# A gated MLP computed in rows instead of columns, and the last rows of its output weight loaded over another weight, beside a decode attention

## The chip, the cores and the metric

One core of a Trainium2 chip. The time is device microseconds of one execution, the median of three runs. The profile is one execution of its own, taken by the hardware profiler. TensorE (PE) multiplies matrices, VectorE (DVE) and ScalarE (ACT) work on lanes, GpSimd (POOL) fills constants, and SyncE (SP) issues nearly all transfers (DMA) in one order.

## The reference, cut to what matters

For four batch rows of 640 values, the output is the input plus an attention over cached keys and values plus a gated MLP, both of the normalised input.

```python
x = A_x                                  # (4, 1, 640)
xn = _layernorm(x)
# attention: 32 heads of 128, 4096 cached positions
q = xn @ wq                              # wq (640, 4096)
p = softmax(q . k_cache * 128 ** -0.5)   # k_cache (4, 32, 4096, 128)
a = (p @ v_cache) @ wo
# gated MLP: F = 1728, Fh = 864
z = _gelu(xn @ w_in)                     # w_in (640, 1728)
z1, z2 = z[..., :Fh], _layernorm(z[..., Fh:])
g = w_sp * z2 + b_sp                     # S = 1: one number each
return x + a + (z1 * g) @ w_out          # w_out (864, 640)
```

The caches are 134 MB each and bfloat16. All weights together are about 14 MB.

## The kernel before, in words

**Units.** The attention is cut into `NU` = 16 units, one batch row and eight heads each. A unit's keys and its values are 8.39 MB each. Keys come in four quarters (`NK`) of 64 KB by 128 lanes in total, into `ring` (shown as k_ring), seven places of a quarter each. Values go to `v_all`, which holds one unit.

**One quarter of keys** (`product`, `fold_half`, `sums`, called by the loop at the end with a running number n): DVE multiplies the quarter by the broadcast query (L537), adds its halves (L543), and PE sums the rest by eight products with the identity (L555). After the sums the ring place is free. `row_sums`, `head_max`, `exps` and `by_head` make the weights of a unit; `weighted` (L631) multiplies them with the values.

**Order of the transfers.** `loads` is a list written out by hand. `pump` goes along it and issues on SP until an entry needs a place that is still in use. The first call of `pump` comes right after the list, before the normalisation and the query products are written down. It issues: unit 0's first and second key quarters, `load_w` (w_in and w_out's large parts), unit 0's other two quarters, `load_w_few` (w_out's 12-lane part). Unit 1's keys need the ring place that unit 0's first quarter holds, so they wait for the `sums` of that quarter. Unit 0's values need `v_all`, marked V, which is freed after the MLP's last step. The tile framework keeps the order in which reads and writes of one place are written down: a later access waits for an earlier one. It also lets transfers take turns on eight completion counters, and a transfer waits for the one eight before it on its counter.

**Places at the start.** `v_all` is first a store for weights: wq in columns 0 to 20,479, w_in in 20,480 to 29,119, then the five-row part of w_out. The other parts of w_out lie in `p_buf` (shown as p_m), which later holds the attention's weights.

**The start of the work.** x comes in by ACT's queue. DVE normalises it (L265 to L274), PE transposes it (L289), and 40 products with wq (L303) make the queries, copied out by L311. `stage_q` spreads a unit's query over the lanes (L519, L527), and the loop begins.

**The MLP** (`gmlp`) is a generator whose pieces the loop places between the first two quarters' steps: after n = 0 the products, after the fold of n = 1 the polynomial and the tanh and the gate with the lane sums, after the sums of n = 1 the statistics, the scale and the output products, and then `v_all` is freed. Before, the MLP has the features on lanes: 140 products (L404) with pieces of w_in as weights give 14 columns by 4 batch rows on up to 128 lanes for each half. The elementwise steps work on 112 values a lane (L414 to L432). The statistics of the normalisation come from a product with ones, a reduction on one lane (L435 to L473), and a product that sends them back to all lanes (L482). L503 multiplies the result with w_out's 14 parts, in two halves of 320 columns each.

Of the kernel before, what the change touches and what calls it, by code (L numbers as in the profile page):

```python
# [9 lines left out]
FP32 = mybir.dt.float32  # L10
BF16 = mybir.dt.bfloat16
# [6 lines left out]
def kernel(  # L18
# [40 lines left out]
    RW = 8  # L59
    QW = HC * Dh  # L60
    RING = 2 * NK - 1
    W_OUT = ((P, 5, 1), (P, 1, 1), (12, 8, 4))
    assert sum(n * r for n, r, _ in W_OUT) == Fh
    NFC = sum(r for _, r, _ in W_OUT)

    def up(n):
        return -(-n // 256) * 256

    PW = sum(up(r * D) for _, r, _ in W_OUT[1:])
    NOH = D // 2  # L70
    CB = 4
    NG = NR // CB
# [26 lines left out]
    ring = places.tile([P, RING, QW], BF16, name="k_ring")  # L99
    x_bf = ring[0:Bsz, 1, 0:D]  # L100
    nc.scalar.dma_start(out=x_bf, in_=A_x.flatten_outer_dims())
    v_all = places.tile([P, NK * QW], BF16, name="v_all")

    wq_sb = v_all[:, 0 : DC * HD].rearrange("p (c n) -> p c n", c=DC)
# [1 line left out]


    at_v = up(DC * (HD + F))
    w_parts, f0, at_p = [], 0, 0
    for n, r, t in W_OUT:  # L110
        if f0 == 0:
            room = v_all[0:n, at_v : at_v + r * D]
        else:
            room = p_buf[0:n, at_p : at_p + r * D]
            at_p += up(r * D)
        w_parts.append((room.rearrange("p (k n) -> p k n", k=r), f0, n, r, t))
        f0 += n * r
    nc.sync.dma_start(out=wq_sb, in_=A_wq.rearrange("(p c) n -> p c n", c=DC))

    def load_part(part):  # L120
        w, f0, n, r, t = part
        rows = B_w_out[f0 : f0 + n * r].rearrange("(p k) n -> p k n", k=r)
        for l in range(t):
            nc.sync.dma_start(out=w[l:n:t], in_=rows[l:n:t])

    def load_w():
        nc.sync.dma_start(out=w_in_sb, in_=B_w_in.rearrange("(p c) n -> p c n", c=DC))
        for part in w_parts:
            if part[4] == 1:
                load_part(part)  # L130

    def load_w_few():
        for part in w_parts:
            if part[4] > 1:
                load_part(part)

    w_rows = [
        (w[:, i], f0 + i, n, r) for w, f0, n, r, _ in w_parts for i in range(r)
    ]

    def run_of(cache, u):
        hg, b = divmod(u, Bsz)
# [137 lines left out]
        op1=ALU.mult,  # L280
    )

    wsp_bf = const.tile([1, 1], BF16)
    bsp_bf = const.tile([1, 1], BF16)

    xn_v = xn_bf.rearrange("b (p c) -> b c p", c=DC)
    xnT_ps = ps_m.tile([P, DC, Bsz], BF16, tag="m")
# [90 lines left out]
            stop=False,  # L378
        )

    gm = {}
    for name in ("zz", "gw", "gt"):
        gm[name] = work.tile([P, 2, NFC, Bsz], FP32, name=name)
    gm["gz"] = work.tile([P, 3, NFC, Bsz], FP32, name="gz")
    nc.gpsimd.memset(gm["zz"][:], 0.0)
    gm["st"] = work.tile([1, 5 * Bsz], FP32, name="st")
    gm["ac"] = work.tile([1, 2 * Bsz], FP32, name="ac")
    gm["yT"] = work.tile([P, NFC, Bsz], BF16, name="yT")

    by_lanes = []  # L390
    for n, r, _ in W_OUT:
        if by_lanes and by_lanes[-1][0] == n:
            by_lanes[-1] = (n, by_lanes[-1][1] + r)
        else:
            by_lanes.append((n, r))

    def gmlp():
        zz, gw, gt, gz = (gm[n] for n in ("zz", "gw", "gt", "gz"))
        zT = ps_pv.tile([P, 2, NFC, Bsz], FP32, tag="pv", name="zT")
        for t in range(2):  # L400
            w_t = w_in_sb[:, :, t * Fh : (t + 1) * Fh]
            for k, (_, f, n, r) in enumerate(w_rows):
                for c in range(DC):
                    nc.tensor.matmul(  # L404
                        out=zT[0:n, t, k, :],
                        lhsT=w_t[:, c, f : f + (n - 1) * r + 1 : r],
                        rhs=xnT[:, c, 0:Bsz],
                        start=(c == 0),
                        stop=(c == DC - 1),
                    )  # L410
        yield
        k0 = 0
        for n, ks in by_lanes:
            nc.vector.tensor_copy(  # L414
                out=zz[0:n, :, k0 : k0 + ks, :], in_=zT[0:n, :, k0 : k0 + ks, :]
            )
            k0 += ks
        nc.vector.tensor_tensor(out=gw[:], in0=zz[:], in1=zz[:], op=ALU.mult)
        nc.vector.tensor_scalar(
            out=gw[:], in0=gw[:], scalar1=0.044715, scalar2=1.0, op0=ALU.mult, op1=ALU.add  # L420
        )
        nc.vector.tensor_tensor(out=gw[:], in0=gw[:], in1=zz[:], op=ALU.mult)
        nc.scalar.activation(
            out=gt[:], in_=gw[:], func=ACT.Tanh, scale=math.sqrt(2.0 / math.pi)
        )
        yield
        nc.vector.tensor_scalar(
            out=gt[:], in0=gt[:], scalar1=1.0, scalar2=0.5, op0=ALU.add, op1=ALU.mult
        )
        nc.vector.tensor_tensor(out=gz[:, 0:2], in0=zz[:], in1=gt[:], op=ALU.mult)  # L430
        sq = gz[:, 2, :, :]
        nc.vector.tensor_tensor(out=sq, in0=gz[:, 1, :, :], in1=gz[:, 1, :, :], op=ALU.mult)  # L432

        s_ps = ps_m.tile([1, 2, NFC, Bsz], FP32, tag="m", name="ln_ps")
        nc.tensor.matmul(  # L435
            out=s_ps[:], lhsT=ones_sq[:, 0:1], rhs=gz[:, 1:3], start=True, stop=True
        )
        yield
        st, ac = gm["st"], gm["ac"]
        mean_t = st[:, 0:Bsz]  # L440
        ex2_t = st[:, Bsz : 2 * Bsz]
        var_t = st[:, 2 * Bsz : 3 * Bsz]
        rst_t = st[:, 3 * Bsz : 4 * Bsz]
        tmp_t = st[:, 4 * Bsz : 5 * Bsz]
        nc.vector.tensor_reduce(
            out=st[:, 0 : 2 * Bsz].rearrange("o (s b) -> o s b", s=2),
            in_=s_ps[:].rearrange("o s k b -> o s b k"),
            axis=AX.X,
            op=ALU.add,
        )  # L450
        nc.vector.tensor_scalar(
            out=st[:, 0 : 2 * Bsz],
            in0=st[:, 0 : 2 * Bsz],
            scalar1=1.0 / float(Fh),
            scalar2=None,
            op0=ALU.mult,
        )
        nc.vector.tensor_tensor(out=tmp_t, in0=mean_t, in1=mean_t, op=ALU.mult)
        nc.vector.tensor_tensor(out=var_t, in0=ex2_t, in1=tmp_t, op=ALU.subtract)
        nc.scalar.activation(  # L460
            out=rst_t, in_=var_t, func=ACT.Sqrt, bias=eps_tile[:1], scale=1.0
        )
        wsp_t = work.tile([1, 1], FP32, name="wsp_t")
        nc.gpsimd.tensor_copy(out=wsp_t[:], in_=wsp_bf[:])
        bsp_t = work.tile([1, 1], FP32, name="bsp_t")
        nc.gpsimd.tensor_copy(out=bsp_t[:], in_=bsp_bf[:])
        yield
        nc.vector.reciprocal(out=rst_t, in_=rst_t)
        nc.vector.tensor_scalar(
            out=ac[:, 0:Bsz], in0=rst_t, scalar1=wsp_t[:, 0:1], scalar2=None, op0=ALU.mult  # L470
        )
        nc.vector.tensor_tensor(out=tmp_t, in0=ac[:, 0:Bsz], in1=mean_t, op=ALU.mult)
        nc.vector.tensor_scalar(  # L473
            out=ac[:, Bsz : 2 * Bsz],
            in0=tmp_t,
            scalar1=-1.0,
            scalar2=bsp_t[:, 0:1],
            op0=ALU.mult,
            op1=ALU.add,
        )  # L480
        ac_ps = ps_m.tile([P, 2 * Bsz], FP32, tag="m", name="ac_ps")
        nc.tensor.matmul(  # L482
            out=ac_ps[:], lhsT=ones_sq[0:1, :], rhs=ac[:], start=True, stop=True
        )
        ac_sb = work.tile([P, 2 * Bsz], FP32, name="ac_sb")
        nc.scalar.copy(out=ac_sb[:], in_=ac_ps[:])
        yield
        nc.vector.tensor_tensor(
            out=sq,
            in0=gz[:, 1, :, :],  # L490
            in1=ac_sb[:, None, 0:Bsz].to_broadcast([P, NFC, Bsz]),
            op=ALU.mult,
        )
        nc.vector.tensor_tensor(
            out=sq,
            in0=sq,
            in1=ac_sb[:, None, Bsz : 2 * Bsz].to_broadcast([P, NFC, Bsz]),
            op=ALU.add,
        )
        nc.vector.tensor_tensor(out=gm["yT"][:], in0=gz[:, 0, :, :], in1=sq, op=ALU.mult)  # L500
        for k, (w, _, n, _) in enumerate(w_rows):
            for half in range(2):
                nc.tensor.matmul(  # L503
                    out=out_sum(half),
                    lhsT=gm["yT"][0:n, k, :],
                    rhs=w[:, half * NOH : (half + 1) * NOH],
                    start=False,
                    stop=False,
                )
        yield  # L510

    qbcs, scores, pvs = {}, {}, {}
# [219 lines left out]
    E = mybir.EngineType  # L732
    with tc.manual_schedule(engines={E.PE, E.DVE, E.Activation, E.SP}):
        stage_q(0)
        nc.scalar.dma_start(out=wsp_bf[:], in_=B_w_sp[0:1, 0:1])
        nc.scalar.dma_start(out=bsp_bf[:], in_=B_b_sp[0:1].rearrange("(a b) -> a b", a=1))
        waiting = None
        mlp = gmlp()
        for n in range(NK * NU):
# [116 lines left out]
```

## Time and profile before

| | us |
|---|---|
| median of three runs (661.91 to 662.43) | 662.18 |
| the profiled execution's own time | 662.09 |
| its span, first to last instruction | 660.2 |
| DVE busy | 522.6 |
| PE busy | 317.0 |
| ACT busy | 29.9 |
| POOL busy | 10.1 |

The span is what the trace covers; the profiled execution's own time is 1.9 us longer. Busy times of engines overlap and do not add up. A transfer's row in the timeline is the time that SP took to issue it, not the time in which its bytes moved; when it landed is read from who waited for it. Transferred are 282.55 MB in all.

### The profile page before, as it was taken

The page shows a single profiled execution, that of the slowest core. Times are in us where ns is not written, and L with a number is a line of the kernel's source. Part 1 is how long each engine was busy: PE and PEld are TensorE (multiplying, and loading weights), DVE is VectorE, ACT ScalarE, POOL GpSimd, SP SyncE. Part 2 cuts the span into 40 slices and gives each one's busy share as a digit, 9 for nine tenths or more (in the row PEclk, how much of TensorE's full clock was granted, in tenths as well). Part 3 has the DMA queues.
Part 4 walks back from the last instruction along what each step waited for, and adds up shares of the span by engine and source line. Part 5 has one row for each costly group of instructions (what it writes and reads, how often), then busy time and mean ns, then how long its engine had stood idle before and what let it go on. Part 6 is the DMA issues. An engine that isn't in the chain of part 4 may idle for free.

```text
span 660.2 us, 4777 instructions
## 1 busy us (share of the span) xinstructions
PE 317.0 (48%) x2083; PEld 136.3 (21%) x2083; DVE 522.6 (79%) x276; ACT 29.9 (5%) x73; POOL 10.1 (2%) x20
## 2 busy tenths in 40 slices
PE   0574372526427363452636336263452534737367
PEld 0231121212213121120212112121120211212124
DVE  1767978959597795969959598695969969999950
ACT  0020000000000000000000000000000000000000
POOL 2300000000000000000000000000000000000000
PEclk9757676766767676585767768676685867676785
DMA  9999999999999999999999999999999999999997
GB/s 369 433 461 434 417 441 434 433 437 438 421 445 426 437 430 441 437 422 433 434 441 441 418 437 441 430 441 421 434 441 437 426 421 445 422 427 436 449 409 284
DMA packets 8232, 282.55 MB, mean 428 GB/s; under 512 B 892, under 2 KB 2184, under 8 KB 2568
## 3 DMA queue, kind: packets, MB, share of 16 engines
q1 hardware_dynamic: 8192, 282.25, 99.1%
q8 instruction: 16, 0.26, 0.1%
q10 hardware_dynamic: 20, 0.01, 0.0%
q14 instruction: 4, 0.03, 0.0%
HBM read 282.24 MB, written 0.01 MB: 428 GB/s over the span
## 4 chain that ended last, share of the span: by engine, by line
DMA 62%; DVE 28%; PE 8%; issue 1%; ACT 0%; DVEq 0%
DMA k_ring<-in_A_k_cache_dram 53%; DVE k_ring L537 14%; DVE k_ring L543 7%; PE s_ps L555 6%; DMA v_all<-in_A_v_cache_dram 4%; DMA k_ring<-in_A_wo_dram 3%; DVE s_sb L569 3%; DMA v_all<-in_A_wq_dram 2%; DVE p_m L607 1%; DVE m L578 1%; PE q_ps L303 1%; PE pv L631 1%; PE out_ps L699 1%; DVE p_m L678 1%; DVE mf L580 1%
## 5 line engine op out<-in xcount | busy, mean ns | idle before, releaser
L537 DVE TENSOR_TENSOR k_ring<-k_ring,qbc 128x8192 bf16<-128x8192 bf16 x64 | 282.9, 4420 | 88.5 <-DMA k_ring<-in_A_k_cache_dram 87.9
L555 PE MATMUL s_ps<-k_ring,ident 128*128 128x512 bf16 x512 | 202.2, 566 | 313.8 <-DVE k_ring L543 313.7
L555 PEld LDWEIGHTS <-ident 128*128 128x128 bf16 x512 | 64.0, 130 | 430.0 <-issue 245.4
L543 DVE TENSOR_TENSOR k_ring<-k_ring 128x4096 bf16<-128x4096 bf16 x64 | 145.9, 2280 | 1.1
L631 PE MATMUL pv<-v_all,p_m 128*32 128x512 bf16 x960 | 62.5, 419 | 0.0
L569 DVE TENSOR_REDUCE s_sb<-s_ps 128x128 f32<-128x1024 f32 x32 | 39.0, 1218 | 3.7 <-PE s_ps L555 3.7
L607 DVE TENSOR_TENSOR p_m<-p_c,own 128x2048 bf16<-128x2048 bf16 x16 | 36.6, 2285 | 0.7 <-ACT p_c L596 0.7
L631 PEld LDWEIGHTS <-p_m 128*32 128x32 bf16 x992 | 26.6, 106 | 42.5 <-issue 23.3
L596 ACT ACTIVATE p_c<-s_sb,nm 128x256 bf16<-128x256 f32 x16 | 8.1, 508 | 342.9 <-DVE nm L588 342.9
L662 PEld LDWEIGHTS o_ps<-o_rows,pick 128*128 128x128 f32 x96 | 20.4, 294 | 4.3 <-issue 3.3
L662 PE MATMUL o_ps<-o_rows,pick 128*128 128x128 f32 x96 | 19.1, 367 | 0.0
L643 ACT COPY o_rows<-pv 128x512 f32<-128x512 f32 x16 | 9.4, 586 | 165.7 <-PE pv L631 165.7
L311 DVE TENSOR_SCALAR q_rows<-q_ps 128x512 bf16<-128x512 f32 x2 | 1.4, 692 | 12.8 <-PE q_ps L303 12.8
L817 DVE TENSOR_TENSOR o_n_last<-o_last,rden_all 128x32 bf16<-128x32 f32 x1 | 0.2, 192 | 12.2 <-PE o_last L809 12.2
L303 PE MATMUL q_ps<-v_all,xnT 128*32 128x512 bf16 x40 | 4.5, 630 | 9.3 <-DMA v_all<-in_A_wq_dram 9.3
L527 ACT CAST qbc<-qbc_ps 128x128 bf16<-128x128 f32 x16 | 4.3, 266 | 97.6 <-PE qbc_ps L519 97.6
L578 DVE TENSOR_REDUCE m<-s_sb 128x1 f32<-128x256 f32 x16 | 6.7, 420 | 0.5
L519 PE MATMUL qbc_ps<-q_rows,of_row 128*128 128x128 bf16 x32 | 6.0, 276 | 0.6 <-DVE q_rows L311 0.6
L519 PEld LDWEIGHTS <-of_row 128*128 128x128 bf16 x32 | 4.1, 132 | 8.1 <-issue 7.4
L716 PE MATMUL o_last<-hot,o_rows 128*128 128x8 f32 x32 | 4.9, 279 | 0.7 <-ACT o_rows L643 0.7
L716 PEld LDWEIGHTS o_last<-hot,o_rows 128*128 128x128 f32 x32 | 4.8, 226 | 1.8 <-ACT o_rows L643 1.6
L699 PE MATMUL out_ps<-k_ring,p_m 128*4 128x320 bf16 x48 | 4.0, 309 | 2.1 <-DVE p_m L691 2.1
(87 smaller groups left out, 81.4 us busy)
## 6 DMA issues: line engine op xcount, KB each, us to landing
k_ring<-in_A_k_cache_dram SPq DMA_DIRECT2D x5, 4096.0 KB, 27.2
v_all<-in_A_v_cache_dram SPq DMA_DIRECT2D x2, 4096.0 KB, 28.2
v_all<-in_A_wq_dram SPq DMA_DIRECT2D x1, 5120.0 KB, 15.4
k_ring<-in_A_k_cache_dram SPq DMA_DIRECT2D x2, 2048.0 KB
k_ring<-in_A_v_cache_dram SPq DMA_DIRECT2D x1, 4096.0 KB
k_ring<-in_A_wo_dram SPq DMA_DIRECT2D x3, 1280.0 KB, 20.6
v_all<-in_B_w_in_dram SPq DMA_DIRECT2D x1, 2160.0 KB
k_ring<-in_A_v_cache_dram SPq DMA_DIRECT2D x1, 2048.0 KB
```

The source lines that it names most:

```text
L303: nc.tensor.matmul(out=q_ps[k * QD : (k + 1) * QD], lhsT=xnT[:, c, :], rhs=wq_v[:, c, k, e], start=(c == 0), stop=(c == DC - 1),)
L519: nc.tensor.matmul(out=qb_ps[:], lhsT=of_row[:, e, b].rearrange("p k f l -> p (k f l)"), rhs=q_rows[e][:, hg, :], start=(e == 0), stop=(e ...
L537: nc.vector.tensor_tensor(out=t, in0=t, in1=qbcs[u][:, None, :].to_broadcast([P, HC, Dh]), op=ALU.mult)
L543: nc.vector.tensor_tensor(out=t[:, :, 0:HD2], in0=t[:, :, 0:HD2], in1=t[:, :, HD2:Dh], op=ALU.add)
L555: nc.tensor.matmul(out=s, lhsT=ident[:], rhs=t[:, :, g * RW : (g + 1) * RW], start=(g == 0), stop=(g == m - 1),)
L569: nc.vector.tensor_reduce(out=scores[u][:].rearrange("p (r c) -> p r c", r=NK)[:, lo : hi + 1 : hi - lo], in_=sums_ps.pop(n // 2)[:], axis ...
L578: nc.vector.tensor_reduce(out=m1[:], in_=scores[u][:], axis=AX.X, op=ALU.max)
L607: nc.vector.tensor_tensor(out=p_m[:, u % 2], in0=p_c.pop(u)[:].rearrange("p (g c) -> p g c", c=CB)[:, :, :, None].to_broadcast([P, NG, CB, HT]
L631: nc.tensor.matmul(out=pvs[u][cg * QD : (cg + 1) * QD, :], lhsT=p_m[:, u % 2, g0 + n].rearrange("p c h -> p (c h)"), rhs=v_at[:, n * CB : ...
L662: nc.tensor.matmul(out=gr[hg][:], lhsT=pick[:, c, Bsz - 1 - b : P + Bsz - 1 - b], rhs=o[:, c, :], start=(b == 0 and c == 0), stop=(b == Bs ...
L699: nc.tensor.matmul(out=out_sum(half), lhsT=o, rhs=wo_sb[:, n, half * NOH : (half + 1) * NOH], start=False, stop=(hg == HG - 1 and n == HT ...
L716: nc.tensor.matmul(out=o_last[0][:, :, :, u % Bsz], lhsT=o[:, c, :], rhs=hot[:, c, :].rearrange("p (k e) -> p k e", e=PAR), start=(c == 0) ...
```

## The change

The MLP's features now lie in rows: the normalised input (four batch rows, padded to 32 columns) is the weight, and w_in streams. Four products side by side fill four groups of 32 lanes with 160 features of each half (`z_w`), and the other 224 features of each half lie on the first 32 lanes (`z_r`). The elementwise steps work on 768 values a lane. ACT sums the values and squares along the lanes, and one product with a 0/1 matrix divided by Fh (`same`) adds over the lane groups and sends the result to all lanes. For the output the result is turned by a block transpose of 32 by 32 blocks (`yb` to `yT`), after which features lie on lanes in groups of four.

w_out's last 224 rows accordingly lie on 16 lanes (two rows each), 15 lanes (eight rows each) and 9 lanes (eight rows each). The 15 and the 9 lanes are three of each four, so each of these parts takes three transfers; with the 16-lane part there are seven transfers instead of five, beside the large part. The 16-lane part lies in `p_buf`. The 15- and 9-lane parts lie in `v_all` from column 0 (home "q"), in the store of wq, and `gw` and `yT` lie behind them. The 15-lane part is loaded with w_in ("first"), the 9-lane part after unit 0's keys ("then"). The loads of w_sp and b_sp move from the loop's start on ACT to right behind x.

```diff
-    W_OUT = ((P, 5, 1), (P, 1, 1), (12, 8, 4))
+    W_OUT = (
+        (P, 5, "v", 4, "first"),
+        (16, 2, "p", 4, "first"),
+        (15, 8, "q", 3, "first"),
+        (9, 8, "q", 3, "then"),
+    )
...
+    places_w = {
+        "v": (v_all, up(DC * (HD + F))),
+        "p": (p_buf, 0),
+        "q": (v_all, 0),
+    }
...
+    def load_part(part, when):
+        w, f0, n, r, used, at = part
+        if at != when:
+            return
+        rows = B_w_out[f0 : f0 + n * r]
+        if used == GAP:
+            nc.sync.dma_start(out=w, in_=rows.rearrange("(p k) n -> p k n", k=r))
         else:
+            by_used = rows.rearrange("(q l k) n -> l q k n", l=used, k=r)
+            for l in range(used):
+                nc.sync.dma_start(out=w[l::GAP], in_=by_used[l])
...
     def gmlp():
-        zT = ps_pv.tile([P, 2, NFC, Bsz], FP32, tag="pv", name="zT")
-            for k, (_, f, n, r) in enumerate(w_rows):
-                for c in range(DC):
+        z_w = ps_pv.tile([P, 2, FN], FP32, tag="pv", name="z_w")
+        for c in range(DC):
+            for g in range(NQ):
+                nc.tensor.matmul(
+                    out=z_w[g * QD : (g + 1) * QD],
+                    lhsT=xnT[:, c, :],
+                    rhs=w_v[:, c, :, g * FN : (g + 1) * FN],
...
+        nc.scalar.mul(out=zz[:, :, 0:FN], in_=z_w[:], mul=0.5)
+        nc.scalar.mul(out=zz[0:QD, :, FN:FW], in_=z_r[0:QD], mul=0.5)
...
+        for i, func in enumerate((ACT.Copy, ACT.Square)):
+            nc.scalar.activation(
+                out=gw[:, i], in_=zz[:, 1], func=func, accum_out=ss[:, i : i + 1]
+            )
...
+        nc.vector.transpose(
+            out=yT.rearrange("p k b -> p (k b)"), in_=yb[:].rearrange("p k b -> p (k b)")
+        )
+        for w, _, _, r, _, _ in w_parts:
+            for i in range(r):
+                for half in range(2):
                     nc.tensor.matmul(
+                        out=out_sum(half),
+                        lhsT=yT[0 : w.shape[0], k, 0:Bsz],
+                        rhs=w[:, i, half * NOH : (half + 1) * NOH],
...
     with tc.manual_schedule(engines={E.PE, E.DVE, E.Activation, E.SP}):
         stage_q(0)
-        nc.scalar.dma_start(out=wsp_bf[:], in_=B_w_sp[0:1, 0:1])
-        nc.scalar.dma_start(out=bsp_bf[:], in_=B_b_sp[0:1].rearrange("(a b) -> a b", a=1))
```

## The prediction, made before the changed kernel was run

> **What bounds the kernel now.** I read the page first: the queues, then the busiest line of DVE.
>
> ```profile
> q1 hardware_dynamic: 8192, 282.25, 99.1%
> HBM read 282.24 MB, written 0.01 MB: 428 GB/s over the span
> L537 DVE TENSOR_TENSOR k_ring<-k_ring,qbc 128x8192 bf16<-128x8192 bf16 x64 | 282.9, 4420 | 88.5 <-DMA k_ring<-in_A_k_cache_dram 87.9
> ```
>
> The sixteen DMA engines are busy 99.1% of the span. DVE, the busiest engine, stands still 88 us before its products because keys have not landed. So the transfers bound the kernel: a microsecond in which no transfer is queued is lost for good, and work that leaves the queue filled costs nothing. I next read SP's rows of the timeline, where transfers are issued, and the chain of waits.
>
> ```profile
> 0.73 0.39 SPq L118 DMA_DIRECT2D v_all<-in_A_wq_dram  x1
> 1.18 1.60 SPq L164 DMA_DIRECT2D k_ring<-in_A_k_cache_dram  x2
> 2.83 0.53 SPq L127 DMA_DIRECT2D v_all<-in_B_w_in_dram  x1
> 3.40 0.50 SPq L124 DMA_DIRECT2D v_all<-in_B_w_out_dram  x1
> 3.95 0.46 SPq L124 DMA_DIRECT2D p_m<-in_B_w_out_dram  x1
> 16.12 0.33 SPq L164 DMA_DIRECT2D k_ring<-in_A_k_cache_dram  x1
> 20.95 7.95 SPq L124 DMA_DIRECT2D p_m<-in_B_w_out_dram  x4
> 32.04 0.34 SPq L164 DMA_DIRECT2D k_ring<-in_A_k_cache_dram  x1
> 46.29 0.33 SPq L175 DMA_DIRECT2D v_all<-in_A_v_cache_dram  x1
> 75.45 0.33 SPq L164 DMA_DIRECT2D k_ring<-in_A_k_cache_dram  x1
> ```
>
> ```profile
> 0.73 15.37 DMA v_all<-in_A_wq_dram
> 16.15 4.48 PE q_ps L303 x31
> 21.95 4.44 DVE k_ring L537
> 28.75 3.26 PE s_ps L555 x8
> 32.04 30.99 DMA k_ring<-in_A_k_cache_dram
> 75.45 26.23 DMA k_ring<-in_A_k_cache_dram
> ```
>
> The chain: wq lands at 16.1, PE makes the queries, DVE the first key quarter's product, PE its sums; only then is a ring place free, and at 32.04 SP issues unit 1's keys (8.39 MB). They land at 63.03. The transfers land in the order of issue at about 433 GB/s: 8.39 MB take 19.4 us, unit 0's values (46.29) then end at 82.4, and unit 2's keys at 82.4 + 19.4 = 101.8, where the chain has 75.45 + 26.23 = 101.7. So at 32.04 the queue had work to about 43, and at 75.45 to 82.4. The start has 11 us of cover, later steps 7.
>
> **The change part by part.** *Where the rows go.* Before, w_out's small parts go to p_m, which nothing uses yet. Now the 15- and 9-lane parts go to columns 0 to 10,239 of v_all, where wq lies. `pump` issues them before the query products are written down, so the program orders them as: wq, these rows over it, then the products. The changed program's list of instructions and waits says so: the first product (now L318) waits for all three 15-lane transfers, the ninth for all three 9-lane ones. Some of wq's lanes are thus overwritten before they are read; for the time, only the wait counts. On PE all 40 products, the queries' spreading, the key sums and everything later stand behind it; DVE's first product waits for PE, and SP's issue of unit 1's keys for both.
>
> *When they are issued.* The list has the first 15-lane transfer wait for w_in too, and SP issues in order, so the second half of unit 0's keys stands behind it. w_in's landing comes from SP's waits:
>
> ```profile
> SPq L164 <- DMA v_all<-in_B_w_in_dram: 2.1, 1, 2.1
> ```
>
> SP had done its four p_m issues at 20.95 + 7.95 = 28.90 and waited 2.1 us more: 31.0. In front of it the queue is unchanged. Issues of this kind stand 0.56 us apart (2.83, 3.40, 3.95), so three give 32.7, where unit 0's last key half is issued (16.12 before); the 9-lane ones follow at 33.0 to 34.2.
>
> *When they land.* A lone transfer needs 2.3 us from issue to use: x is issued at 0.73, and this row starts at 3.02:
>
> ```profile
> 3.02 0.45 PE L373 MATMUL out_ps<-k_ring,ident 4*32 4x320 bf16 x2 [3.02 <-DMA k_ring<-in_A_x_dram]
> ```
>
> The queue holds w_out until 32.9, so the key half (4.19 MB, 9.7 us) lands at 32.7 + 2.3 + 9.7 = 44.7. The nine-lane rows stand behind it: 9 rows of 10 KB. Spread over all engines they take 92 KB / 433 = 0.2 us; all on one engine (433 / 16 = 27 GB/s) 3.4. A mean packet has 282.55 MB / 8232 = 34 KB, so a row is nearer to one packet on one engine; three transfers of three rows then take 3 x 10.2 KB / 27 = 1.1. I take 45.8.
>
> A rule of the Trainium skill would spread them unevenly for good: DMA: Bandwidth & Descriptors, section "Why a DMA increments its semaphore by 16 and not by 1", says that a transfer uses the largest count of engines up to 16 that divides its outer size, the lowest-numbered ones. By that rule engines 0 to 2 carry 61 KB of the small lane parts instead of 41 KB, less 8 KB saved on the former 128-lane part, 0.5 us at 27 GB/s, and the sum below would be 684.3 instead of 683.8; no run here resolves single engines.
>
> *To unit 1's keys.* Eight of the 40 products run early; 32 remain at 4.48 / 40 = 0.112: 3.6 us, end 49.4. From the products' end to the first DVE product was 21.95 - 20.63 = 1.3: 50.7, that is 28.8 later than before. The issue of unit 1's keys follows at 32.04 + 28.8 = 60.8, with the queue empty since 45.8. They land at 60.8 + 2.3 + 19.4 = 82.5 instead of 63.03: **19.5 us late**. This alone is the floor of the loss.
>
> *The MLP itself.* 140 products of 128x4 (4.6 us) become 25 of 320 and 448 columns. Query products of 512 columns take 0.43 per four side by side; by columns that is 5 x 0.27 + 5 x 0.37 = 3.2 us, from 61.2 (sums and spreading, 32.4 + 28.8) to 64.4. The second fold ends at 35.4 + 28.8 = 64.2. ACT's copy of the rest adds 0.5 (128x512 takes 0.586): DVE starts at 64.9. The pieces after it, from these rows:
>
> ```profile
> L422 DVE TENSOR_TENSOR gw<-gw,zz 128x112 f32<-128x112 f32 x1 | 0.3, 275 | 0.0
> L500 DVE TENSOR_TENSOR yT<-gz 128x56 bf16<-128x56 f32 x1 | 0.2, 219 | 0.0
> L687 DVE STREAM_TRANSPOSE p_m<-p_m 128x256 bf16<-128x256 bf16 x3 | 1.3, 445 | 0.1
> ```
>
> The first two give 0.16 + 0.001 per element. Three passes over 768: 2.9. Tanh on 768 about 1.0 (296 ns for 112, 508 for 256, 586 for a copy of 512). Two ACT sums over 384 with their read-outs, 1.3. Lane sums on PE 0.4; two small DVE steps 0.35. Square root's table (1.28) starts when the sums end, so it adds 0.5, and the root 0.3. Three small steps 0.6, the scaling of 384 0.4, four products of 32 to 160 elements 1.1, the transpose of 736 between 1.0 and 1.3. Sum 10.0 with the gaps: DVE is free at 74.9, where it was at 44.62: 30.3 late. Then 46 output products instead of 28; ten took 1.5 us, so 6.9, and unit 0's values are issued at about 81.8 (46.29 before). Alone in the queue they would start at 84.1, against 82.5 behind unit 1's keys; they land at 103.5.
>
> *Who is late next.* DVE. Unit 0's last fold ended at 59.03; now 89.3, after unit 1's keys have landed. From the start of unit 1's first product to unit 2's key issue were 75.45 - 63.06 = 12.4: issue at 101.7, landing at max(101.7 + 2.3, 103.5) + 19.4 = 123.4, against 101.7: **21.7 late**. Unit 1 keeps DVE 94.96 - 63.06 = 31.9 us, to 121.2, before that landing, so DVE has caught up. From there the queue is full as before and the lateness stays: no row before the end has idle transfers to give it back.
>
> *Costed at nothing:* the earlier loads of w_sp and b_sp (a few bytes on ACT, which idles until 4.20); POOL's larger fills (it idles from 5.5 to 27); the same w_out bytes in fewer, longer rows. The 128-lane part had 160 KB, 0.4 us at 433; half to twice that bounds the gain, and it lies before 33 us, inside the queue's cover.
>
> **Sum.** The profiled execution took 662.09 (span 660.2), 0.09 under the median of 662.18. 662.1 + 21.7 = 683.8, rounded to 684.
>
> **The rivals.**
> 1. *The rows wait for the products instead* (the other side). If the overwriting transfers were held until the query products have read wq (20.6), or the products were not held, SP would issue the key half at about 22 and unit 1's keys at 32 still; the queue has work to 33 and then 43. The longer MLP (values issued near 55, needed by 63) is hidden too: 662.1, give or take 0.5. It decides if the products end before about 29 us, since 29 + 11.4 to the key issue + 2.3 meets the queue's end at 43. The list of waits speaks against it; for it speaks only that the diff itself names no wait. Chance 0.04.
> 2. *Only unit 1's keys are late.* If the MLP takes 2 us less or PE runs its output products twice as fast, DVE is not the later one: 662.1 + 19.5 = 681.6, and 680 if the nine-lane rows cost 0.2. Chance 0.27; DVE's pieces above speak against it.
> 3. *The small transfers are slower.* On one engine each (3.4 us), with an issue twice as long (+1.7): 684 + 4 = 688. Nothing in the rows shows it. Chance 0.14.
> 4. *A gain from the longer rows*, with rival 1's order and 1.4 us or more from 128 fewer short rows: 660.6. That is over three times the whole part's 0.4 us: chance 0.02.
>
> **How the numbers follow.** My forecast, 684 (682 to 686.5), has 0.53; its neighbours 2 and 3 are slower too: slower 0.94, same 0.04, faster 0.02. 0.2%, 1.3 us, is about what a measurement of this kernel can tell from no change. The range takes in rival 2's lower end with two microseconds for a quicker start (678) and rival 3 with a longer MLP (690).
>
> **What would show it.** In the changed profile: the first query products at about 34, a gap on PE to 45 or 46 put down to w_out's transfers, and their end near 49; key issues at 32.7, 60.8 and 101.7 in SP's rows; a stretch of 45 to 62 with nearly no bytes; keys landing near 82.5 and 123; the same rows as before from there on, 22 us later. I am wrong if the query products run by 21 us, if bytes flow between 46 and 60, or if the lateness at unit 3's keys differs from that at the end.

## The result, and the profile after

The changed kernel takes 686.88 us (median of four runs, 686.31 to 687.53) against 662.04 for the kernel before, a ratio of 1.0376 (95% interval 1.0363 to 1.0388): 24.8 us slower. The forecast was 684, in a range of 678 to 690. The profiled execution took 687.43 with a span of 685.6, 25.4 more than before.

SP's rows of the changed kernel's timeline, where the transfers are issued (start, time to issue, tile and source):

```profile
3.62 0.45 SPq L143 DMA_DIRECT2D p_m<-in_B_w_out_dram  x1
30.89 2.29 SPq L147 DMA_DIRECT2D v_all<-in_B_w_out_dram  x3
33.22 0.44 SPq L181 DMA_DIRECT2D k_ring<-in_A_k_cache_dram  x1
33.70 2.09 SPq L147 DMA_DIRECT2D v_all<-in_B_w_out_dram  x3
62.68 0.34 SPq L181 DMA_DIRECT2D k_ring<-in_A_k_cache_dram  x1
82.74 0.33 SPq L192 DMA_DIRECT2D v_all<-in_A_v_cache_dram  x1
102.42 0.33 SPq L181 DMA_DIRECT2D k_ring<-in_A_k_cache_dram  x1
```

From 4.07 to 30.89 SP issues nothing: it waits 26.7 us for w_in, with unit 0's second key half behind that wait (33.22, before 16.12). Unit 1's keys are issued at 62.68 instead of 32.04. Why they are late stands in PE's rows, all engines' timeline of the same kernel:

```profile
35.18 1.04 PE L318 MATMUL q_ps<-v_all,xnT 128*32 128x512 bf16 x8 [28.55 <-DMA v_all<-in_B_w_out_dram]
47.46 3.46 PE L318 MATMUL q_ps<-v_all,xnT 128*32 128x512 bf16 x32 [11.24 <-DMA v_all<-in_B_w_out_dram]
52.27 4.42 DVE L564 TENSOR_TENSOR k_ring<-k_ring,qbc 128x8192 bf16<-128x8192 bf16 x1 [0.60 <-ACT qbc L554]
```

The brackets are the point: eight query products wait 28.55 us, until the 15-lane rows of w_out have landed, and the other 32 wait 11.24 us more for the 9-lane rows, although the first 12 MB, with wq in front, moved as before (table below). They then read a wq that those rows have partly overwritten. What that does to the transfers is in the windows (the first columns are busy times by engine; the last two are the share of the DMA engines that was busy, and GB/s; both count a packet wholly in the window in which it begins, so a share can exceed 1):

```profile
32.00:34.00 2.00, 0.00 (x0) 0.00 (x0) 0.00 (x0) 0.00 (x0) 0.00 (x0) 1.00 0.21 61
34.00:44.00 10.00, 1.04 (x8) 0.17 (x8) 0.00 (x0) 0.00 (x0) 0.00 (x0) 1.00 1.04 420
44.00:48.00 4.00, 0.54 (x8) 0.33 (x12) 0.00 (x0) 0.00 (x0) 0.00 (x0) 1.00 0.08 31
48.00:62.00 14.00, 6.23 (x41) 2.13 (x33) 11.08 (x5) 0.27 (x1) 0.00 (x0) 0.72 0.00 0
62.00:82.00 20.00, 13.64 (x85) 6.07 (x85) 15.68 (x19) 7.34 (x12) 0.00 (x0) 0.59 1.00 417
```

From 48 to 62 us no packet begins, and from 44 to 48 only the nine overwriting rows, one packet of keys and marks of 4 bytes do. The trace's records of single packets give the edges: nothing moves from 47.0 to 63.65 us. Summing the bytes of one-microsecond windows in both kernels gives how much later the changed kernel has moved the same amount:

| MB moved | 12 | 14 | 17 | 25 | 28 | 40 | 180 | 282 |
|---|---|---|---|---|---|---|---|---|
| us later | -0.1 | 2.9 | 21.7 | 22.4 | 23.4 | 24.0 | 24.6 | 24.7 |

So 21.7 us are lost before unit 1's keys flow, and 2.3 more by 40 MB, near the end of unit 2's keys. From there on the lateness stays between 23.8 and 25.0: the stream runs as before. The page's queue line shows it as a share:

```profile
q1 hardware_dynamic: 8104, 282.25, 95.9%
L564 DVE TENSOR_TENSOR k_ring<-k_ring,qbc 128x8192 bf16<-128x8192 bf16 x64 | 282.8, 4419 | 82.4 <-DMA k_ring<-in_A_k_cache_dram 81.8
```

The same bytes now keep the DMA engines busy for 95.9% of the span (99.1% before), and DVE's work is the same: 64 products in 282.8 us.

### The profile page after: what moved, and what is told of

Same layout as the page of the kernel before. It is cut to its first block, busy times and chain, and to the rows that moved or that the text cites. A ratio compares the mean times of both kernels' runs of the same rounds, so it can differ in the third digit from the quotient of the medians.

```text
span 685.6 us, 4589 instructions
## 1 busy us (share of the span) xinstructions
PE 313.0 (46%) x1986; PEld 132.8 (19%) x1986; DVE 525.2 (77%) x271; ACT 32.2 (5%) x78; POOL 6.0 (1%) x22
## 3 DMA queue, kind: packets, MB, share of 16 engines
q1 hardware_dynamic: 8104, 282.25, 95.9%
## 4 chain that ended last, share of the span: by engine, by line
DMA 59%; DVE 30%; PE 8%; issue 1%; SPq 1%; ACT 1%; DVEq 0%
DMA k_ring<-in_A_k_cache_dram 46%; DVE k_ring L564 15%; DVE k_ring L570 7%; PE s_ps L582 6%; DMA v_all<-in_B_w_in_dram 4%; DMA v_all<-in_A_v_cache_dram 4%; DMA k_ring<-in_A_wo_dram 3%; DVE s_sb L596 3%; DMA v_all<-in_B_w_out_dram 2%; DVE p_m L634 1%; DVE m L605 1%; PE pv L658 1%; DVE p_m L705 1%; PE out_ps L726 1%; SPq L147 1%
## 5 line engine op out<-in xcount | busy, mean ns | idle before, releaser
L564 DVE TENSOR_TENSOR k_ring<-k_ring,qbc 128x8192 bf16<-128x8192 bf16 x64 | 282.8, 4419 | 82.4 <-DMA k_ring<-in_A_k_cache_dram 81.8
L658 PE MATMUL pv<-v_all,p_m 128*32 128x512 bf16 x960 | 61.0, 411 | 0.0
L689 PE MATMUL o_ps<-o_rows,pick 128*128 128x128 f32 x96 | 19.5, 370 | 0.0
L318 PEld LDWEIGHTS <-xnT 128*32 128x32 bf16 x40 | 1.4, 131 | 42.2 <-issue 30.1
L529 PE MATMUL out_ps<-v_all 20*4 20x320 bf16 (+2 forms) x42 | 6.0, 467 | 0.6 <-DVE v_all L522 0.6
```

Source lines behind the costliest of these rows:

```text
L564: nc.vector.tensor_tensor(out=t, in0=t, in1=qbcs[u][:, None, :].to_broadcast([P, HC, Dh]), op=ALU.mult)
L658: nc.tensor.matmul(out=pvs[u][cg * QD : (cg + 1) * QD, :], lhsT=p_m[:, u % 2, g0 + n].rearrange("p c h -> p (c h)"), rhs=v_at[:, n * CB : ...
L689: nc.tensor.matmul(out=gr[hg][:], lhsT=pick[:, c, Bsz - 1 - b : P + Bsz - 1 - b], rhs=o[:, c, :], start=(b == 0 and c == 0), stop=(b == Bs ...
```

## The experiments

Theory A: the query products wait for rows that are written over wq ahead of them, the wait holds back unit 1's keys, and the transfers run dry. Theory B: the MLP in rows itself costs the time. Theory C: w_out in more and smaller transfers costs it. Later runs ask what remained.

### One part done without the other: the MLP in rows, the overwriting held back

```diff
-        (16, 2, "p", 4, "first"),
-        (15, 8, "q", 3, "first"),
-        (9, 8, "q", 3, "then"),
+        (16, 14, "q", 4, "late"),
...
         q_rows.append(rows)
+    for part in w_parts:
+        load_part(part, "late")
```

> The changed kernel, but w_out's last 224 rows lie on 16 lanes of 14 rows each, come in one transfer, and that transfer is written down after the query products, so it waits for them and they wait for nothing but wq. The MLP in rows, the lane sums and the block transpose stay as they are (38 output products). Theory A (the loss is the query products' wait for the overwriting rows): the products run at 16 to 20.6 us again, unit 1's keys are issued at 32, unit 0's values near 51 and thus before those keys have landed; the queue never runs dry and the time is 662 us, 661 to 663. Theory B (the MLP in rows itself costs the time, by its longer passes on DVE and its later release of the value place): most of the 25 us stays, 675 to 687. Theory C (w_out in small transfers on few engines costs the stream): about 662 too, but then the next two kernels, which keep the small transfers, tell it from A.

664.53 us, ratio 1.0038 (1.0025 to 1.0051). The new MLP is all there, and 22 of the 25 us are gone: theory B falls as the account of the loss. PE's and SP's rows of the timeline:

```profile
16.09 4.38 PE L316 MATMUL q_ps<-v_all,xnT 128*32 128x512 bf16 x40 [9.58 <-DMA v_all<-in_A_wq_dram]
19.72 0.34 SPq L141 DMA_DIRECT2D v_all<-in_B_w_out_dram  x1
32.22 0.34 SPq L179 DMA_DIRECT2D k_ring<-in_A_k_cache_dram  x1
50.97 0.33 SPq L190 DMA_DIRECT2D v_all<-in_A_v_cache_dram  x1
```

The products wait for wq alone, unit 1's keys are issued at 32.22, the values at 50.97, well before the keys have landed. But the time is 1.5 us above the upper end expected; that is taken up below.

### The other part alone: the old MLP, its 12-lane rows over wq

```diff
+        elif t > 1:
+            room = v_all[0:n, 0 : r * D]
         else:
             room = p_buf[0:n, at_p : at_p + r * D]
```

> The kernel before with its old MLP and its old four transfers of the 12-lane part; only the place of that part is changed, from p_m to the first columns of v_all, over wq, as the changed kernel does with its 15- and 9-lane parts. As there, the queries come from a wq that is partly overwritten. Theory A: the four transfers stand behind unit 0's second key half, land near 45, and hold all 40 query products (45.5 to 50); unit 1's keys are issued near 61.5 instead of 32.0, the queue is dry from 44 to 63, and the time is 662 + 21 = 683, 681 to 685. The old MLP is shorter, so unit 0's values come early enough and little is added after that. Theory B: no new MLP, so 662, 661 to 664. Theory C: the transfers are those of before, so 662.

684.55 us, ratio 1.0339 (1.0324 to 1.0355). Nothing of the new MLP is there, and the four transfers are those of before; only their place has moved. This is what separates A from C. The groups of PE's waits name it:

```profile
PE q_ps L305 <- DMA v_all<-in_B_w_out_dram: 37.6, 1, 37.6
```

The issue of unit 1's keys, from SP's rows:

```profile
59.63 0.35 SPq L166 DMA_DIRECT2D k_ring<-in_A_k_cache_dram  x1
```

61.5 was expected; the first product started at 43.9 and not at 45.5.

### The 9-lane rows ahead of the key half

```diff
-        (9, 8, "q", 3, "then"),
+        (9, 8, "q", 3, "first"),
```

> The changed kernel, but the 9-lane part is loaded ahead of unit 0's second key half, not behind it; wq is overwritten before it is read, as in the changed kernel. Theory A: the 9-lane rows land near 37.3 instead of 47.4, the query products end near 41, unit 1's keys are issued near 52.6 instead of 62.7, and all later issues follow 10 us earlier: 662 + 14.6 = 676.7, 675 to 679. Theories B and C: the MLP and the number of transfers are unchanged, so 687, 685 to 688.

677.50 us, ratio 1.0234 (1.0220 to 1.0248). One word of the diff gives back 9.4 us. The query products' second part starts at 38.1 instead of 47.5, unit 1's keys are issued at 53.52 instead of 62.68: 9.2 us earlier, and the span is 9.7 shorter.

```profile
53.52 0.33 SPq L181 DMA_DIRECT2D k_ring<-in_A_k_cache_dram  x1
```

### The changed kernel without the MLP

```diff
     def gmlp():
-        w_v = w_in_sb.rearrange("p c (t f) -> p c t f", t=2)
...
+        for _ in range(6):
+            yield
```

> The changed kernel without the MLP's computation (products, elementwise steps, statistics, transpose and output products are left out, the output lacks the MLP's term); all transfers and the query products' wait for them stay. Theory A: unit 1's keys are still issued at 62.7 and land near 84.5 instead of 63, 21.5 us late; unit 0's values are issued at once behind them and DVE is ready in time, so only the few us that the MLP adds behind the keys go away: 662 + 21.5 = 683.5, 682 to 685. Theory B: without the MLP the loss is gone, 660 to 665. Theory C: 687.

685.76 us, ratio 1.0361 (1.0345 to 1.0377): 1.1 less than the changed kernel (the single times, 684.59 to 687.56, overlap with its own), 0.8 above what A gave and far from B. In this profile the overwriting rows landed later, and the keys were issued at 64.72, so the times are better compared from that issue on, as the table below does. This kernel also shows a term that the others hide, because here DVE waits for unit 1's keys (chain of waits: start, length):

```profile
64.72 21.74 DMA k_ring<-in_A_k_cache_dram
```

8.39 MB into an empty queue take 21.74 us from issue to use, where the prediction worked out 2.3 + 19.4 = 21.7.

### Both small parts behind the key half

```diff
-        (15, 8, "q", 3, "first"),
+        (15, 8, "q", 3, "then"),
```

> The changed kernel, but the 15-lane part too is loaded behind unit 0's second key half, so that half is issued as soon as wq has landed (16 us) and the first thin stretch of the stream, around 33 us, is gone; wq is overwritten before it is read, as in the changed kernel. Theory A1 (only the time of unit 1's key issue counts, since the queue is empty before it in any case): the overwriting rows land near 47 as before, unit 1's keys are issued within 1 us of 62.7, and the time is 685.5 to 687.5. Theory A2 (each stretch without bytes costs by itself): the 3.0 us by which the stream fell back around 33 us come back, 683.5 to 684.5.

683.76 us (683.56 to 685.92), ratio 1.0329 (1.0313 to 1.0345). By the times this lies with A2, by the profile with A1: in the profiled execution, which was the slowest of the four at 685.92, the rows landed at 46.0 rather than 47.4, and unit 1's keys were issued at 61.20, 1.5 us earlier; the span is 1.5 shorter than the changed kernel's (684.1 and 685.6). A1's mechanism held, but its number for the landing did not, so the time alone decides nothing. The table over all kernels with a late key issue does:

| kernel | keys of unit 1 issued | span | span after the issue |
|---|---|---|---|
| before (the queue is full at the issue) | 32.04 | 660.2 | 628.2 |
| changed | 62.68 | 685.6 | 622.9 |
| both parts behind the key half | 61.20 | 684.1 | 622.9 |
| 9-lane rows ahead of the key half | 53.52 | 675.9 | 622.4 |
| old MLP, 12-lane rows over wq | 59.63 | 682.6 | 623.0 |
| changed, without the MLP | 64.72 | 685.8 | 621.1 |

Once the queue has run dry, the span is the issue of unit 1's keys plus 622.4 to 623.0 us, whatever MLP stands in the kernel and whatever the stream did before. Taking the MLP out saves 1.8, by one profile of each kernel; the old MLP in its place (623.0) costs as much as the new one.

### What remains: 2.5 us in the held kernel

The stream of the kernel with 16 held lanes fell 2 us behind between 40 and 46 us, while its 287 KB of w_out moved. The next two kernels change where these rows land.

> As the kernel of one held transfer, but the 224 rows lie on 32 lanes of seven rows each, not on 16 of 14 (24 output products instead of 38). That kernel was 2.5 us slower than before, and its stream fell back by 2 us while these 287 KB moved, between 40 and 46 us. Theory P (rows that land on few lanes move slowly and hold up the stream behind them): twice the lanes halve the loss, 662.05 + 1 = 663.1, 662.6 to 663.7. Theory Q (the loss is the transfer's place between the two key loads, or the MLP's longer passes): 664.5, 664.0 to 665.0. The Trainium skill has a figure for this: SBUF - State Buffer, section on the DMA port swizzle, says that the bandwidth goes by the ports that the lanes reach, 27.2 GB/s each; 16 lanes reach four and 32 lanes eight, which would make 2.6 and 1.3 us of these 287 KB against 0.7 over all.

```diff
-        (16, 14, "q", 4, "late"),
+        (32, 7, "q", 4, "late"),
```

663.33 us, ratio 1.0021 (1.0012 to 1.0030), as theory P had it.

> The kernel of one held transfer on 16 lanes, but the same 224 rows land on 112 lanes of two rows each, while the output products still read 16 lanes: the MLP's term of the output is thus computed from other data in its last 224 rows. Work on every engine is the same, only where the 287 KB land differs. Theory P: no loss in the stream, 662.0, 661.6 to 662.6. Theory Q: 664.5, 664.0 to 665.0.

```diff
+            if n == 16:
+                w, r = v_all[0:112, 0 : 2 * D].rearrange("p (k n) -> p k n", k=2), 2
             nc.sync.dma_start(out=w, in_=rows.rearrange("(p k) n -> p k n", k=r))
```

663.00 us, ratio 1.0015 (1.0007 to 1.0024). With the same work on every engine, 112 lanes instead of 16 save 1.5 us: Q falls as the account of that part, and P is right in kind. The windows of the kernel with 16 lanes, and then of the one with 112:

```profile
42.00:44.00 2.00, 2.00 (x6) 0.76 (x5) 1.43 (x6) 1.58 (x2) 0.00 (x0) 0.50 1.69 468
44.00:46.00 2.00, 1.70 (x7) 0.37 (x7) 1.97 (x4) 0.00 (x0) 0.00 (x0) 0.50 0.09 33
```

```profile
42.00:44.00 2.00, 2.00 (x6) 0.69 (x5) 1.39 (x7) 1.58 (x2) 0.00 (x0) 0.50 0.91 343
44.00:46.00 2.00, 1.70 (x8) 0.38 (x8) 1.97 (x4) 0.00 (x0) 0.00 (x0) 0.50 1.18 500
```

The 33 GB/s do not mean that the DMA engines stand still: the packets that began before 44 us were still moving. With each packet's bytes spread over its own time, as the packet records give it, all engines are busy from 41 to 46 us, but at 264 GB/s on 16 lanes, 340 on 32 and 385 on 112, against 433 in the kernel before. On 16 lanes the first key packet of each engine behind the rows takes 2.8 to 4.2 us for its 64 KB, on 112 lanes up to 3.0, where 2.42 is usual. The stream loses 2.0, 1.1 and 0.6 us in this stretch, of 2.5, 1.4 and 1.0 in the time. P expected 662.0, and 1.0 us stays; whether the transfer's place has a share in that is open.

The next kernel is the version that the findings point to: no row over wq, and rows on all lanes where possible.

```diff
+        (P, 6, "v", 4, "first"),
+        (32, 3, "p", 4, "first"),
...
+            pieces = [(v_all, at_v, 0, 5), (p_buf, 0, 5, 6)]
```

> The MLP in rows with another split of w_out: six rows on each of 128 lanes (five in v_all, the sixth in p_m) and the last 96 rows on 32 lanes of three rows in p_m, so that nothing is written over wq and nothing has to be held; 18 output products, passes over 576 values a lane instead of 768. Theory A: the query products run at 16, unit 1's keys are issued at 32, the time is that of the kernel before, 661.3 to 662.5. Theory P adds at most 0.5 for the 123 KB on 32 lanes, less what the 12-lane part of before cost. Theory B (the MLP in rows costs): above 663.

662.78 us, ratio 1.0013 (1.0004 to 1.0022): within 0.2% of the kernel before, 0.3 above the range expected of A, and it does not beat it. From 41 to 46 us its stream runs at 431 GB/s. Two more runs ask whether these last 0.8 us are the MLP's or the transfers'.

```diff
-        for l in range(t):
-            nc.sync.dma_start(out=w[l:n:t], in_=rows[l:n:t])
+        nc.sync.dma_start(out=w, in_=rows)
```

> The kernel before, but its 12-lane part comes in one transfer of 12 lanes, not in four of three. The kernels in rows that hold or avoid the overwriting still stand 0.8 to 1.0 us over the kernel before. Theory R (this rest comes from how w_out's small parts are cut into transfers): 662.3 to 662.8. Theory S (it comes from the MLP in rows): 662.0, 661.8 to 662.2. By the rule of the Trainium skill on how many engines a transfer uses (DMA: Bandwidth & Descriptors, section on the semaphore's increment by 16), the 12 rows would lie on 12 engines of one row each instead of three engines of four rows.

663.70 us, ratio 1.0025 (1.0015 to 1.0035), 1.8 us over its kernel before: the old MLP, the same 12 lanes and 123 KB, one transfer instead of four. R's direction, over twice its size. The packet records show the difference: as four transfers, the 12 rows move in three chains of four, 0.38 us a row, and unit 1's key packets of 64 KB beside and behind them keep their 2.42 us. As one transfer all 12 begin together, between 41.4 and 41.7 us, and 14 such packets that begin from 41.4 to 42.5 take 3.1 to 3.6 us.

> The kernel with nothing over wq, without the MLP's computation (products, elementwise steps, statistics, transpose and output products are left out, the output lacks the MLP's term); all transfers stay. Theory R: the transfers make the rest, 662.8 stays, 662.5 to 663.1. Theory S: the rest is the MLP's work in rows, 662.0 or less, 661.2 to 662.2.

662.76 us, ratio 1.0014 (1.0005 to 1.0023). Leaving out the whole MLP changes 662.78 by 0.02. So this MLP in rows, with 8.5 us of steps on DVE (before: 8.0), costs nothing where the queue is full. By the run before, the cut of w_out's small parts can make a rest of this size; that it makes this one is not shown, since the earlier loads of w_sp and b_sp were not tested alone. Which property of a cut matters (lanes reached, engines used, the place in the queue) these runs don't separate.

## Why the prediction was right, and where its sizes were off

**The bound** was read rightly: in the profiled execution the stream fell back by 24.7 us and the span grew by 25.4, although PE, DVE and ACT together had almost the same work (DVE 522.6 us before, 525.2 after). The measured 686.88 lies inside the range, but 2.9 above the forecast and just above the band of 682 to 686.5 that had been given a chance of 0.53: two terms of the sum were too small.

**The wait and its place.** The first eight products at 35.2 (forecast: about 34), the gap put down to w_out's transfers, the end at 50.9 (49.4), the key issues at 33.2, 62.7 and 102.4 (32.7, 60.8, 101.7), the values at 82.7 (81.8), the first use of unit 2's keys at 126.5 (123.4). The 12-lane rows over wq, with the old MLP, show that such a wait alone costs 22.5 us.

**The landing of the overwriting rows** is the first term that was too small: the products that wait for it went on at 47.46 instead of 45.8. The rows themselves took what was forecast: by the packet records three engines moved three rows each, 0.38 us a row, 1.15 us in all. They began late. SP's three issues of such rows took 2.29 and 2.09 us, 0.73 each, where 0.56 was taken from the start, so the key half was issued 0.5 us late. On the three engines with the rows its last packets ended at 45.1, 45.7 and 45.84, where the forecast had 44.7; the last row ended at 47.0, and 0.46 us later the product began. The key sums took 3.57 instead of 3.26. Together the key issue came 1.9 us later than forecast. This landing also differs from one kernel to the next (46.0, 47.4 and 49.3 in three kernels with the same rows). In the last of them, the one without the MLP, one of the three engines ended its share of the key half only at 47.73; why it lagged was not found.

**The empty queue's 21.7 us** to land 8.39 MB was right (21.74 where it can be seen). What was missing is what follows. In the kernel without the MLP the next two loads, already queued, were used 40.0 us later (product starts 86.56 and 126.54), where before two such loads took 101.7 - 63.03 = 38.7. These 1.3 us are not a slow start: the stream ran at 434 GB/s from 70 to 98 us. By the packet records 17.2 MB moved in the 40.0 us (430 GB/s), against 16.8 MB in the 38.7 before (434); the extra 0.4 MB make 0.9 of the 1.3 us. They come from how a landing is seen: a load is used when the last of its sixteen engines is done, and by then the others have begun the next load. Before, the engines ended unit 1's and unit 2's keys 2.0 us apart each time; here they ended the first 0.5 us apart (85.6 to 86.1) and the second 1.5 (124.5 to 126.0). Unit 3's keys add 0.8 more (39.4 us after unit 2's, before 38.6). Counted from the key issue, the forecast gave 660.2 + 21.7 - 60.8 = 621.1, the changed kernel 622.9. The two terms, 1.9 and 1.8, make the 3.7 us by which its span exceeds the forecast.

**The MLP.** From DVE's start to its end the new MLP took 65.98 to 76.14, 10.2 us (forecast 10.0), the output products 76.27 to 82.66, 6.4 (6.9). Its share behind the keys was put at 21.7 - 19.5 = 2.2; taking it out saved 1.8. But the old MLP at this place costs the same 1.8 (623.0 against 621.1), so this is the price of an MLP behind the wait, not of its form in rows.

**The rivals.** The first, that the rows wait for the products, is what the held kernels make by hand, with one transfer instead of seven: 664.5 and 663.3, not 662.1, since the price of rows on few lanes was not in it. The second (681.6) gave the MLP too little. The third (688) is 1.1 us above the result, nearer to it than the forecast, but not for its reason: the issue took 0.6 us longer, not 1.7, and the rows took 1.15 us, not 3.4. The fourth, a gain from longer rows, shows in no run: the held kernels, without the 128 short rows, took 1.0 to 2.5 us more than before.

**The rule on engines**, DMA: Bandwidth & Descriptors of the Trainium skill, "Why a DMA increments its semaphore by 16 and not by 1", was given 0.5 us here. The packet records agree with its count of engines: the 9-lane rows moved on three, and the 12 lanes in one transfer on twelve, where the four transfers of before used three. They don't name the engines, and no run shows the 0.5 us by themselves. The 12 lanes in one transfer were 1.8 us slower, so spreading rows over more engines is not a gain by itself.

## What to carry to other kernels

Where transfers bound the kernel, ask of an edit when the queue next runs empty, not how much work it adds: with the queue full, leaving out a whole MLP of 8.5 us of steps saved 0.02 us, and the place of one small part of a weight cost 22.5. Before a buffer is used twice, look in which order its writes and reads are written down: a load put into the list ahead of the old contents' readers makes those readers wait for it, and changes what they read. A small load that holds up an engine belongs ahead of a large one in the queue: the 9 lanes alone, moved ahead of 4 MB, gave back 9.4 us.

## What the runs showed of the hardware that was not expected

Few lanes are slow to fill, and hold up what is queued behind them. The kernels with the same 287 KB at the same place in the queue took 2.5 us more than the kernel before on 16 lanes, 1.4 on 32 and 1.0 on 112. The Trainium skill has a rule for the direction (SBUF - State Buffer, section on the DMA port swizzle: bandwidth goes by the ports that the lanes reach, 27.2 GB/s each). By its figures the step from 16 to 32 lanes is 1.3 us, an estimate, and 1.2 was measured; from 32 to lanes that reach all ports it is 0.65, and 0.3 was measured. In the stream alone, from 41 to 46 us, the two steps are 0.9 and 0.5. That the slowing reaches the next transfer is shown by its packets: with all engines busy, 64 KB of keys take up to 4.2 us behind the 16 lanes, where 2.42 is usual. One transfer of 12 lanes in place of four of three cost 1.8 us more. There, too, the key packets are the slow ones (3.1 to 3.6 us), two of them on engines that moved no row just before; with three engines at a time on the rows none is. Why many engines on few lanes slow the packets behind them was not tried.
